# Late tiles of attention and the first Fourier products: sums, differences and splits put at other places

## The chip, the core and the metric

The kernel runs on one core of a Trainium2 chip. The metric is the device time of one execution in microseconds (us), from the first instruction of the core to the last, with what the launch adds around them. Lower is better. Five engines work side by side, each through its own queue in order: TensorE (PE; its weight loads are listed as PEld), VectorE (DVE), ScalarE (ACT), GpSimd (POOL), and SyncE (SP), which here issues the DMAs.

## What is computed

Four layers on `x` of 2048 rows and 640 columns, all in float32: attention, Fourier mixing, attention, Fourier mixing.

```python
def _A_ref(x, wqkv, wo):            # 32 heads of 20 columns
    q, k, v = split(x @ wqkv)
    scores = q @ k.T * 20 ** -0.5   # masked to 0 <= i - j < 256
    return softmax(scores) @ v @ wo
def _B_ref(x, seq_re, seq_im, hid_re, hid_im):
    a, b = x @ hid_re.T, x @ hid_im.T
    return seq_re @ a - seq_im @ b
x = x + _A_ref(_layernorm(x), wqkv, wo)
x = x + _B_ref(_layernorm(x), ...)
x = x + _A_ref(_layernorm(x), wqkv, wo)
x = x + _B_ref(_layernorm(x), ...)
```

## The kernel before

**Numbers in two parts.** A float32 operand of a matmul is split into an upper part (ACT copies it to a shorter format, L176) and a lower part (the difference, on DVE or POOL, L182; helper `split`). A product is then three matmuls: upper times upper, upper times lower, lower times upper. So every operand costs one instruction on ACT and one on DVE or POOL before PE can use it.

**The end of attention.** After the heads the output projection is finished in 16 *late tiles* of 128 rows (`late`, from L1049). For each, PE makes two halves of 320 columns in two accumulator banks; DVE adds each half to the partial result (L1096), which frees its bank, then takes mean and variance (`stats`, L234 to L238, and L1102); POOL takes the inverse root (L1107), ACT normalizes (L1060, L1057), and the row block is split for the next layer (`split_x`: upper part on ACT, lower part on POOL). POOL also makes sums of two row blocks j and j + 8 (`sum1`, L1185, and `sum3`, L1189).

**The Fourier layer** multiplies the DFT matrix of the rows with the normalized `x` (`seq`; matmuls at L1407). With the matrix and `x` each cut into two by two blocks, seven products take the place of eight, so sums and differences of blocks are operands. Each of four parts of the result (two halves of the rows, real and imaginary) takes the eight blocks j = 0 to 7 in three groups of units: "a", "b" and "g". A unit needs a *block* of the DFT matrix (1024 columns by DMA, a first part p and a second part q, raw in one of few buffers) and an *x part*:

- group a: p, and the difference t1 = q - p (L1313);
- group b: q, and q - p (L1321);
- group g, the third: q, then t1 = p - t1 (L1325 or L1337), then t1 - q (L1329 or L1338); three operands, all to be split. For j below 2 in the first part both differences are on DVE; otherwise the first is on POOL (L1337).

`cut_to(n)` makes and splits the block of all units up to n, `x_to(n)` the x parts, `load_to(n)` starts the loads. `seq(n)` calls them for n + 1 first, issues the matmuls of unit n, and then calls `cut_to(n + 2)`.

In the **first part** (sb = part = 0) the units begin while late tiles are still coming: group a is taken apart into "a1" (eight units with p, 9 matmuls each) and "a2" (eight with t1, 9 each). They alternate with late tiles: 12 matmuls of 320 columns for a tile, then 9 of 512 columns for a unit. Group b there has two units "b7" of 9 matmuls, two "b5" of 6, and six "b" of 15. Group g has eight of 21. The x part of a b unit needs the sums of `sum4_to` (two instructions on DVE, L1197 and L1198, for each j), made when `x_to` comes to it.

**What sets the order.** The program is written out in one pass. `post(d, f)` holds f back until the d-th tick after, and ticks come with the matmuls issued (`spend`). So the place of an instruction in its engine's queue is fixed at build; at run time an engine waits at its head. The last heads run under `poll_late(n)`, with n = 15 at their last step.

The ring of eight places for split blocks begins with four slices of `qp[1]`, which holds queries of the last heads until then.

Of the kernel before, what the change touches and what calls it, by code (L numbers as in the profile page):

```python
# [7 lines left out]
F32 = mybir.dt.float32  # L8
# [3 lines left out]
AF = mybir.ActivationFunctionType  # L12
OP = mybir.AluOpType
# [12 lines left out]
NB = S // P  # L26
# [31 lines left out]
def cuts(ap, n):  # L58

    return [ap[:, i:i + n] for i in range(0, ap.shape[1] - n + 1, n)]  # L60
# [6 lines left out]
class Net:  # L67
# [956 lines left out]
    def poll_late(self, n):  # L1024

        if n == 1:
            self.late_w = pairs(cuts(self.qp[0][:, :4 * D], D))
            self.late_c = self.take_cc()
            spare = [t[:, :D] for t in self.late_c[:2]]
            self.late_raw = spare  # L1030
            for k in range(EARLY, KC):
                self.nc.sync.dma_start(spare[k - EARLY], self.a["wo"][:, k, :])
        if 3 <= n < 7:
            (hi, lo), r = self.late_w[(n - 3) // 2], self.late_raw[(n - 3) // 2]
            cs = slice(n % 2 * 320, n % 2 * 320 + 320)
            self.split(hi[:, cs], lo[:, cs], r[:, cs])
        if n == 4:
            self.take_fourier()
            self.load_to(1)
        if n == 15:  # L1040
            self.cut_to(0)
        sb = len(self.late_o)
        if (n > 6 and sb < NSB and (NQ - 1, sb) in self.stored and (self.after or sb < 3)
                and (sb < 3 or self.late_t >= 3) and not (0 < sb < 3 and self.late_o[-1].get("scaled", 0) < KC - EARLY)):
            self.late_load()
# [5 lines left out]
    def late(self, xsrc, xdst, hook):  # L1051
        nc = self.nc
# [28 lines left out]
        for t in range(NB):  # L1081
            sb, i = t // 4, t % 4
            y = self.y_part(t)
# [7 lines left out]
            else:  # L1091
                for hf, cs in enumerate(both):
                    p = self.bank("o", 320)
# [26 lines left out]
            if t == NB - 2:  # L1120
                u = self.last_a2 - 1
                self.post(3, lambda u=u: self.staged(u, 0, nc.vector))
                self.post(6, lambda u=u: self.staged(u, 1))
                self.post(9, lambda u=u: self.staged(u, 2))
            hook(t)
            self.late_t = t + 1
            yield 0
# [86 lines left out]
    def take_fourier(self):  # L1214
        def halves(t):
            return t.rearrange("p (l c) -> p l c", l=2)
# [13 lines left out]
                      for ph, j in (first if sb + part == 0 else  # L1230
                                    [(ph, j) for ph in ("a", "b", "g") for j in range(half)])]
        self.kept = {}
        self.raw_of, self.cut_of, self.x_of = {}, {}, {}
        self.n_raw, self.n_load, self.n_cut, self.n_x = 0, 0, 0, 0
        self.ring = deque((t[:, 0], t[:, 1]) for t in [halves(t) for t in cuts(self.qp[1], 1024)])
        self.free = deque([0, 1, 2, 3, 4, 7])
        self.un, self.normed, self.n_sum = 0, 0, 0
        self.acc = {}
# [48 lines left out]
    def cut_to(self, n):  # L1287
        nc = self.nc
        while self.n_cut <= min(n, len(self.order) - 1):
# [17 lines left out]
            def cut(x, out=out):  # L1307
                c = self.ring.popleft()
                self.ring.append(c)
                self.split(c[0], c[1], x)  # L1310
                out.append(c)
            if ph in ("a", "a1"):
                (nc.vector if first else nc.gpsimd).tensor_tensor(out=t1, in0=q, in1=p, op=OP.subtract)  # L1313
                src = [p] + ([t1] if ph == "a" else [])
            elif ph == "a2":
                src = [t1]
            elif ph == "b5":
                self.cut_of[u] = [self.kept.pop(j)]
                continue
            elif ph == "b":  # L1320
                nc.vector.tensor_tensor(out=p, in0=q, in1=p, op=OP.subtract)  # L1321
                src = [q, p]
            elif first and j < 2:
                cut(q)
                nc.vector.tensor_tensor(out=t1, in0=p, in1=t1, op=OP.subtract)  # L1325
                cut(t1)

                def rest(p=p, q=q, t1=t1, cut=cut):
                    nc.vector.tensor_tensor(out=p, in0=t1, in1=q, op=OP.subtract)  # L1329
                    cut(p)  # L1330
                if j == 0:
                    self.rest_g = rest
                else:
                    rest()
                src = []
            else:
                nc.gpsimd.tensor_tensor(out=t1, in0=p, in1=t1, op=OP.subtract)  # L1337
                nc.vector.tensor_tensor(out=p, in0=t1, in1=q, op=OP.subtract)  # L1338
                src = [q, t1, p]
# [4 lines left out]
    def x_to(self, n):  # L1344
        nc = self.nc
        while self.n_x <= min(n, len(self.order) - 1):
# [23 lines left out]
            if ph == "g":  # L1370
                if first and j == 0:
                    self.xring = [self.work.tile([P, 2, D], F32R, name="xc", tag="wc") for _ in range(2)]
                x = [self.xring[j % 2], self.vq[j % 2].rearrange("p (l c) -> p l c", l=2)]
                self.parts(x[0], b, 0)
                self.parts(x[1], a[:, :256], 0)
            self.x_of[u] = x

    def seq(self, n):
# [46 lines left out]
            mul("m4", x[0], 384, 256, c[2])  # L1425
        soon = last and ph == "b" and not sb + part
        if soon:
            self.gather(sb, part, ph)
            self.rest_g()
            self.x_to(n + 2)  # L1430
        self.cut_to(n + 2)
        if last and not soon:
# [435 lines left out]
```

## Time and profile before

| what | value |
|---|---|
| median of 3 runs | 2134.83 us (2133.2 to 2140.98) |
| the profiled execution | 2135.22 us |
| its span, first to last instruction | 2133.2 us |
| granted clock of PE | 0.999 |
| busy: DVE | 1592.4 us, 75% |
| busy: ACT | 1149.4 us, 54% |
| busy: POOL | 854.3 us, 40% |

So 2.0 us of the profiled execution lie outside its span. In the timeline a row gives start, duration, engine, line, operation, output and inputs, shapes, and the count of merged instructions; in brackets stands how long the engine had been idle before it and what ended that. In the chain a row gives start, duration, engine, tile and line. Starts are what to count with: a new matmul starts before the one ahead of it has left the array, so the distance of two starts is the rate, and the duration is longer.

The code in question runs twice: once in the second layer (about 500 to 650 us) and once in the fourth (about 1560 to 1710 us).

### The profile page before, as it was taken

The page shows a single profiled execution, that of the slowest core. Times are in us where ns is not written, and L with a number is a line of the kernel's source. Part 1 is how long each engine was busy: PE and PEld are TensorE (multiplying, and loading weights), DVE is VectorE, ACT ScalarE, POOL GpSimd, SP SyncE. Part 2 cuts the span into 40 slices and gives each one's busy share as a digit, 9 for nine tenths or more (in the row PEclk, how much of TensorE's full clock was granted, in tenths as well). Part 3 has the DMA queues.
Part 4 walks back from the last instruction along what each step waited for, and adds up shares of the span by engine and source line. Part 5 has one row for each costly group of instructions (what it writes and reads, how often), then busy time and mean ns, then how long its engine had stood idle before and what let it go on. Part 6 is the DMA issues. An engine that isn't in the chain of part 4 may idle for free.

```text
span 2133.2 us, 45011 instructions
## 1 busy us (share of the span) xinstructions
PE 2089.0 (98%) x16405; PEld 1737.8 (81%) x16405; DVE 1592.4 (75%) x3936; ACT 1149.4 (54%) x2511; POOL 854.3 (40%) x975
## 2 busy tenths in 40 slices
PE   8999999999999999999999999999999999999999
PEld 7987776677778888889999877776777788888899
DVE  7448788777887968777751588887788868788787
ACT  3228877766554545543431288787755545445432
POOL 2036666864432324130230466668633334241300
PEclk9999999999999999999999999999999999999999
DMA  6556667876346454667645566778753364556653
GB/s 211 169 150 208 203 202 214 237 234 194 129 123 192 139 168 136 226 202 248 216 142 186 148 201 210 207 221 247 226 189 126 120 194 123 183 161 201 231 173 121
DMA packets 220061, 395.12 MB, mean 185 GB/s; under 512 B 37824, under 2 KB 84416, under 8 KB 219840
## 3 DMA queue, kind: packets, MB, share of 16 engines
q1 hardware_dynamic: 219840, 392.25, 59.3%
q8 instruction: 129, 2.11, 0.4%
q14 instruction: 92, 0.75, 0.1%
HBM read 273.94 MB, written 117.05 MB: 183 GB/s over the span
## 4 chain that ended last, share of the span: by engine, by line
PE 81%; DVE 6%; POOL 4%; DMA 4%; ACT 3%; issue 1%; SPq 0%; ACTq 0%; POOLq 0%; DVEq 0%
PE banks L1407 29%; PE banks L189 15%; PE banks L207 13%; PE banks L703 7%; PE banks L1662 7%; PE banks L661 5%; PE banks L629 5%; DMA rr<-r_d 1%; POOL big L182 1%; POOL ou L1337 1%; DVE banks L634 1%; DVE qp L182 1%; PE banks L289 1%; ACT big L1057 1%; DMA pt<-c 1%
## 5 line engine op out<-in xcount | busy, mean ns | idle before, releaser
L634 DVE CUSTOM_DVE_ANT_0 banks<-banks,mask 128x384 f32<-128x384 f32 (+2 forms) x1024 | 513.8, 565 | 147.7 <-PE banks L629 119.0
L672 ACT ACTIVATE pt<-banks 128x384 f32<-128x384 f32 (+2 forms) x864 | 359.7, 472 | 74.1 <-PE banks L629 32.7
L629 PE MATMUL banks<-kp,qp 60*128 60x384 f32 (+2 forms) x1024 | 336.7, 368 | 4.7 <-DVE mc L634 2.9
L207 PE MATMUL banks<-big,wc 64*128 64x512 f32 x1920 | 337.0, 396 | 0.4 <-DVE pt L422 0.4
L661 PE MATMUL banks<-qp,kp 61*128 61x384 f32 (+2 forms) x1024 | 334.4, 362 | 2.7 <-DMA qp<-mt 1.1
L629 PEld LDWEIGHTS banks<-kp,qp 60*128 60x128 f32 x1024 | 172.0, 184 | 59.6 <-DVE mc L634 44.0
L661 PEld LDWEIGHTS banks<-qp,kp 61*128 61x128 f32 x1024 | 176.6, 185 | 41.7 <-ACT pt L672 16.0
L686 POOL TENSOR_SCALAR_AFFINE_SELECT pt<-pt 128x512 f32<-128x512 f32 x216 | 138.3, 640 | 172.4 <-ACT pt L672 142.4
L207 PEld LDWEIGHTS banks<-big,wc 64*128 64x128 f32 x1920 | 196.5, 187 | 12.2 <-DVE pt L422 0.5
L1337 POOL TENSOR_TENSOR pt<-pt,pt 128x512 f32<-128x512 f32 x36 | 62.0, 1721 | 288.7 <-DMA pt<-c 148.9
L176 ACT ACTIVATE cc<-pt 128x512 fp32r<-128x512 f32 x150 | 93.9, 626 | 153.9 <-POOL pt L1313 52.5
L703 PE MATMUL banks<-pt,vq 128*32 128x128 f32 (+1 forms) x3664 | 172.0, 311 | 3.7 <-POOL pt L686 3.7
L176 ACT ACTIVATE qp<-pt 128x512 fp32r<-128x512 f32 (+1 forms) x195 | 119.8, 624 | 93.4 <-DVE pt L1338 45.6
L182 DVE TENSOR_TENSOR cc<-pt,cc 128x512 fp32r<-128x512 f32 x150 | 121.4, 820 | 52.0 <-ACT cc L176 49.7
L182 DVE TENSOR_TENSOR qp<-pt,qp 128x512 fp32r<-128x512 f32 (+1 forms) x195 | 151.7, 791 | 10.5 <-ACT qp L176 7.9
L1407 PE MATMUL banks<-qp,big 128*128 128x512 f32 x630 | 151.1, 391 | 5.0 <-DVE qp L182 4.0
L703 PEld LDWEIGHTS banks<-pt,vq 128*32 128x32 f32 x3664 | 97.6, 109 | 60.4 <-issue 16.9
L634 DVE DVE_READ_ACCUMULATOR2_ANT mc<- 128x1 f32 x1024 | 144.6, 141 | 0.0
L1407 PEld LDWEIGHTS banks<-qp,big 128*128 128x128 f32 x630 | 117.0, 188 | 31.1 <-DVE qp L182 5.7
L690 POOL TENSOR_SCALAR_AFFINE_SELECT pt<-pt 128x512 f32<-128x512 f32 x190 | 123.0, 648 | 0.0
L1407 PE MATMUL banks<-qp,xc 128*128 128x512 f32 x480 | 117.9, 390 | 1.8 <-DVE xc L182 1.5
L1407 PEld LDWEIGHTS banks<-qp,xc 128*128 128x128 f32 x480 | 89.8, 188 | 22.2 <-DVE xc L182 2.3
(240 smaller groups left out, 4529.1 us busy)
## 6 DMA issues: line engine op xcount, KB each, us to landing
pt<-c SPq DMA_DIRECT2D x188, 512.0 KB
kp<-qk_d SPq DMA_DIRECT2D x128, 160.0 KB
qp<-qk_d SPq DMA_DIRECT2D x128, 160.0 KB
kp<-u_d SPq DMA_DIRECT2D x32, 640.0 KB
o_d<-ou SPq DMA_DIRECT2D x64, 256.0 KB
x_d<-x SPq DMA_DIRECT2D x48, 320.0 KB
v_d<-pt SPq DMA_DIRECT2D x16, 768.0 KB
qk_d<-cc SPq DMA_DIRECT2D x24, 512.0 KB
```

What stands on the lines that cost most here:

```text
L176: nc.scalar.activation(hi, src, AF.Copy, scale=-1.0 if neg else 1.0)
L182: (eng or nc.vector).tensor_tensor(out=lo, in0=src, in1=hi.bitcast(F32), op=OP.subtract)
L189: self.nc.tensor.matmul(p, x, y, start=n == 0, stop=n == last)
L207: self.nc.tensor.matmul(ps[a], x[r], y[r], start=half + i == 0, stop=half == 1 and i == n - 1, skip_group_check=True)
L629: nc.tensor.matmul(p, qp[quad % 2][b:b + 60, z, qb * P:(qb + 1) * P], kp[quad % 2][b:b + 60, z, k0 * P:(qb + 1) * P], start=True, stop=True)
L634: nc.vector.tensor_tensor_reduce(out=p, in0=p, in1=self.mask[:, 384 - n * P:], scale=1.0, scalar=NEG, op0=OP.add, op1=OP.max, accum_out=mc ...
L661: nc.tensor.matmul(self.banks[:, tb[e], :n * P], kp[quad % 2][b:b + 61, z, kb * P:(kb + 1) * P], qp[quad % 2][b:b + 61, z, kb * P:(kb + n) ...
L672: nc.scalar.activation(pt[quad, kb][:, 2 * z + e, :n * P], self.banks[:, tb[e], :n * P], AF.Exp, scale=SCALE)
L686: nc.gpsimd.affine_select(out=t[:, :, 0:P], in_=t[:, :, 0:P], pattern=[[0, h], [1, P]], compare_op=OP.is_ge, fill=0.0, base=0, channel_mul ...
L703: nc.tensor.matmul(p[32 * h:32 * h + 32, (c0 - qa) * P:(c1 - qa) * P], vq[:, 96 * (kb % 4) + 21 * h:96 * (kb % 4) + 21 * h + 32], t[:, h, ...
L1407: nc.tensor.matmul(self.banks[:, bk, :], p, b[q], start=start and m == 0, stop=stop and last and m == 2, skip_group_check=True)
L1662: nc.tensor.matmul(bank[to], a, b, start=start and n == 0, stop=stop and n == last, skip_group_check=True)
```

## The change

It touches only the late tiles and the first part of each Fourier layer.

1. At the last step of the heads `cut_to(1)` takes the place of `cut_to(0)`, so the blocks of the first two a1 units are split there. The ring takes the slices of `qp[1]` in the order 0, 2, 1, 3.
2. The first two differences t1 (j = 0 and 1) are not made there: they are kept in `put_off` and posted with late tiles 7 and 8.
3. The sums of `sum4_to` for j = 0 to 4 are posted with late tiles 8 to 12; for j = 5 to 7 they stay in `x_to`.
4. In group g of the first part all differences are on DVE, for every j (before, POOL made the first one from j = 2 on). The upper parts are issued with new helpers `upper` (ACT) and `lower` (DVE), and in another order: both differences are queued before the second lower part.
5. In group g the x part of unit n + 2 is issued ahead of the block of unit n + 2, at the end of `seq(n)`. At the end of group b, the x part of the second g unit has its upper parts issued ahead of the sums that gather group b, and its lower parts (`rest_x`) behind the rest of the first g block.

```diff
         if n == 15:
-            self.cut_to(0)
+            self.cut_to(1)
...
                 self.post(9, lambda u=u: self.staged(u, 2))
+            if 0 <= t - NB // 2 < 5:
+                self.post(9, lambda j=t - NB // 2: self.sum4_to(j + 1))
+            if t in (7, 8,):
+                self.post(9, self.put_off.pop(0))
             hook(t)
...
-        self.ring = deque((t[:, 0], t[:, 1]) for t in [halves(t) for t in cuts(self.qp[1], 1024)])
+        self.ring = deque((t[:, 0], t[:, 1]) for t in [halves(cuts(self.qp[1], 1024)[i]) for i in (0, 2, 1, 3)])
...
+            def upper(x, out=out):
+                c = self.ring.popleft()
+                self.ring.append(c)
+                nc.scalar.activation(c[0], x, AF.Copy)
+                out.append(c)
+
+            def lower(i, x, out=out):
+                nc.vector.tensor_tensor(out=out[i][1], in0=x, in1=out[i][0].bitcast(F32), op=OP.subtract)
             if ph in ("a", "a1"):
-                (nc.vector if first else nc.gpsimd).tensor_tensor(out=t1, in0=q, in1=p, op=OP.subtract)
+                def less(j=j, t1=t1, p=p, q=q, first=first):
+                    (nc.vector if first else nc.gpsimd).tensor_tensor(out=t1, in0=q, in1=p, op=OP.subtract)
+                    if first:
+                        self.lessened.add(j)
+
+                if first and j < 2:
+                    self.put_off.append(less)
+                else:
+                    less()
...
-            elif first and j < 2:
-                cut(q)
+            elif first:
+                upper(q)
+                lower(0, q)
                 nc.vector.tensor_tensor(out=t1, in0=p, in1=t1, op=OP.subtract)
-                cut(t1)
-
-                def rest(p=p, q=q, t1=t1, cut=cut):
-                    nc.vector.tensor_tensor(out=p, in0=t1, in1=q, op=OP.subtract)
-                    cut(p)
+                upper(t1)
+                nc.vector.tensor_tensor(out=p, in0=t1, in1=q, op=OP.subtract)
+                lower(1, t1)
+                upper(p)
                 if j == 0:
-                    self.rest_g = rest
+                    self.rest_g = lambda p=p, lower=lower: lower(2, p)
                 else:
-                    rest()
+                    lower(2, p)
                 src = []
...
-                self.parts(x[0], b, 0)
-                self.parts(x[1], a[:, :256], 0)
+                for d, y in zip(x, (b, a[:, :256])):
+                    if not (first and j == 1):
+                        self.parts(d, y, 0)
+                    else:
+                        nc.scalar.activation(d[:, 0], y, AF.Copy)
+                        self.rest_x.append(lambda d=d, y=y: nc.vector.tensor_tensor(
+                            out=d[:, 1], in0=y, in1=d[:, 0].bitcast(F32), op=OP.subtract))
...
         if soon:
+            self.rest_x = []
+            self.x_to(n + 2)
             self.gather(sb, part, ph)
             self.rest_g()
+            for f in self.rest_x:
+                f()
+        if ph == "g" and not sb + part and j in (0,1,2,3,4,5,):
             self.x_to(n + 2)
         self.cut_to(n + 2)
```

In the changed kernel the lines move: L1313 becomes L1328, L1197 and L1198 become L1201 and L1202, L1321 becomes L1344, L1337 becomes L1360, L1407 becomes L1435, L1456 becomes L1489; the lower parts of group g stand at L1325, and its two differences at L1349 and L1351.

In the listings of the order below, a row is one instruction in an engine's queue (line, operation, output and inputs, shape of the output, and a count where equal ones follow); minus is before only, plus is changed only. `pt_96` and `vq_92` are places of t1, `s_6559` and `s_6560` raw blocks (later sums), `cc`, `rr` and `qp_102` places of split blocks, `xc` and `vq` of x parts.

## The prediction on record

> **What bounds the kernel now.** I read the page first: span, busy shares and chain.
>
> ```profile
> span 2133.2 us, 45011 instructions
> PE 2089.0 (98%) x16405; PEld 1737.8 (81%) x16405; DVE 1592.4 (75%) x3936; ACT 1149.4 (54%) x2511; POOL 854.3 (40%) x975
> PE 81%; DVE 6%; POOL 4%; DMA 4%; ACT 3%; issue 1%; SPq 0%; ACTq 0%; POOLq 0%; DVEq 0%
> ```
>
> TensorE is the bound, so only its stalls can be won: 2133.2 - 2089.0 = 44 us, and a few tenths after each restart that count as busy. The edits lie where the chain leaves PE. So next came PE's timeline over the first Fourier part in the second layer, with only the rows that matter kept:
>
> ```profile
> 517.23 2.45 PE L1407 MATMUL banks<-qp,big 128*128 128x512 f32 x10
> 520.99 2.11 PE L1407 MATMUL banks<-qp,big 128*128 128x512 f32 x8 [1.31 <-DVE qp L182]
> ...
> 535.35 2.03 PE L189 MATMUL banks<-qp,kp 128*128 128x320 f32 x12 [0.78 <-DVE x L1096]
> ...
> 569.17 0.73 PE L1407 MATMUL banks<-qp,big 128*128 128x512 f32 x2 [0.72 <-DVE qp L182]
> ...
> 575.27 2.21 PE L1407 MATMUL banks<-qp,big 128*128 128x512 f32 x9
> ...
> 603.88 2.20 PE L1407 MATMUL banks<-qp,xc 128*128 128x512 f32 x9
> ...
> 646.43 3.79 PE L1407 MATMUL banks<-qp,big 128*128 128x512 f32 x16
> ```
>
> and the same places in the fourth layer:
>
> ```profile
> 1634.84 2.20 PE L1407 MATMUL banks<-qp,big 128*128 128x512 f32 x9
> ...
> 1663.45 2.20 PE L1407 MATMUL banks<-qp,xc 128*128 128x512 f32 x9
> ...
> 1706.65 1.52 PE L1407 MATMUL banks<-qp,big 128*128 128x512 f32 x6
> ```
>
> Last, the chain in order of time, for the rate when nothing waits and for what stands behind the worst stall of the third group:
>
> ```profile
> 614.10 4.33 DMA pt<-c
> 618.56 3.63 POOL ou L1337
> 622.21 1.77 DVE pt L1338
> 627.67 264.87 PE banks L1407 x1167
> ```
>
> An unhindered 512-column matmul takes 264.87 / 1167 = 0.227 us. From 575.27 to 603.88 PE issues 9 + 9 + 2 x 6 + 6 x 15 = 120 matmuls: 27.24 us of work in 28.61, so **1.37 us lost in group b**; the fourth layer (1634.84 to 1663.45) loses the same. Group g has 8 x 21 = 168: 38.14 us in 42.55 (603.88 to 646.43), so **4.41 lost in group g**, and 43.20 - 38.14 = 5.06 in the fourth layer. The second unit should have started at 517.23 + 10 x 0.227 = 519.50 and came at 520.99: 1.49 lost.
>
> **Part 1: the second unit's block, split within the heads.** DVE's queue behind the late tiles, at the start of the second unit:
>
> ```order
>  L1102 TENSOR_SCALAR nb<-mv 128x1
> -L1313 TENSOR_TENSOR pt_96<-s_6560 128x512
> -L182 TENSOR_TENSOR qp_102<-s_6560,qp_102 128x512
> -L1313 TENSOR_TENSOR pt_96<-pt_95 128x512
> +L1328 TENSOR_TENSOR pt_96<-pt_95 128x512
>  L182 TENSOR_TENSOR qp_102<-pt_95,qp_102 128x512
> ```
>
> Two instructions are gone from here; inside the heads one L182 takes the place of one L1313. Their price, and what a late tile costs DVE:
>
> ```profile
> 519.12 1.21 DVE L1313 TENSOR_TENSOR pt<-s 128x512 f32<-128x512 f32 x1
> 520.25 0.68 DVE L182 TENSOR_TENSOR qp<-s,qp 128x512 fp32r<-128x512 f32 x1
> 520.86 0.68 DVE L1313 TENSOR_TENSOR pt<-pt 128x512 f32<-128x512 f32 x1
> ...
> 534.82 0.88 DVE L1096 TENSOR_TENSOR x<-banks,big 128x320 f32<-128x320 f32 x2
> ...
> 536.97 0.68 DVE L1313 TENSOR_TENSOR pt<-pt 128x512 f32<-128x512 f32 x1
> 537.57 0.68 DVE L182 TENSOR_TENSOR cc<-pt,cc 128x512 fp32r<-128x512 f32 x1
> ...
> 540.92 1.51 DVE L182 TENSOR_TENSOR cc<-pt,cc 128x512 fp32r<-128x512 f32 x1
> 542.36 0.88 DVE L1096 TENSOR_TENSOR x<-banks,big 128x320 f32<-128x320 f32 x2
> ...
> 548.61 0.81 DVE L182 TENSOR_TENSOR qp<-pt,qp 128x512 fp32r<-128x512 f32 x1 [0.90 <-ACT qp L176]
> 549.34 0.88 DVE L1096 TENSOR_TENSOR x<-banks,big 128x320 f32<-128x320 f32 x2
> ...
> 561.04 0.88 DVE L1096 TENSOR_TENSOR x<-banks,big 128x320 f32<-128x320 f32 x2
> ```
>
> From 519.12 to 520.86 the two take 1.74 us; with the collision that a later L1313 avoids I take 2.0 (1.7 to 2.1). The rows up to 542.36 bear no bracket, that is, no idle time ahead of them, so all of DVE's work there comes 2.0 earlier. PE's stall at 520.99 goes (1.49), and of the one at 535.35, which waits for DVE's L1096, what makes 2.0 together. The upper part that moves into the heads is one more ACT instruction in their last step; ACT is busy 54% of the span, and I cost it at nothing. Uncovered, it would be of the size of DVE's 0.68 for as many columns.
>
> **Part 2: differences and sums behind late tiles.** DVE's queue at tiles 8 to 10:
>
> ```order
>  L182 TENSOR_TENSOR cc<-pt_95,cc 128x512
> +L1328 TENSOR_TENSOR pt_96<-s_6559 128x512
> +L1096 TENSOR_TENSOR x<-banks,big_5491 128x320 x2
> +L234 BN_STATS st<-x 128x6 x2
> +L236 BN_AGGR mv<-st 128x2
> +L238 TENSOR_SCALAR rs<-mv 128x1
> +L1102 TENSOR_SCALAR nb<-mv 128x1
> +L182 TENSOR_TENSOR cc<-pt_96,cc 128x512
> +L1201 TENSOR_TENSOR big_5460<-big_5460 128x256
> +L1202 TENSOR_TENSOR kp_7441<-big_5491,big_5460 128x256
> +L1328 TENSOR_TENSOR pt_96<-s_6560 128x512
>  L1096 TENSOR_TENSOR x<-banks,big_5491 128x320 x2
> ```
>
> Each of five tiles gets a pair of sums, two of them a difference as well, all ahead of the next L1096, which frees the bank that the next late tile's matmuls need. A difference is 0.60 (536.97 to 537.57). The pair, from group b's rows:
>
> ```profile
> 577.09 0.42 DVE L1197 TENSOR_TENSOR big<-big 128x256 f32<-128x256 f32 x1
> 577.54 0.43 DVE L1198 TENSOR_TENSOR kp<-big,big 128x256 f32<-128x256 f32 x1
> 577.88 0.42 DVE L1197 TENSOR_TENSOR big<-big 128x256 f32<-128x256 f32 x1
> ```
>
> is 0.79. DVE waits 0.90 per tile for ACT here (548.61), so alone the pair would fit. But POOL is busy at the same time:
>
> ```profile
> 540.35 1.53 POOL L182 TENSOR_TENSOR big<-big,big 128x384 fp32r<-128x384 f32 x1 [1.51 <-ACT big L176]
> ...
> 548.13 0.74 POOL L1185 TENSOR_TENSOR big<-big,big 128x256 f32<-128x256 f32 x1 [0.65 <-ACT big L1057]
> 549.44 0.74 POOL L182 TENSOR_TENSOR big<-big,big 128x256 fp32r<-128x256 f32 x1 [0.57 <-ACT big L176]
> ```
>
> At 540.92 DVE's L182 took 1.51 instead of 0.68 while POOL's L182 ran, until 541.88: it waited for POOL's whole instruction. At 548.61 it took 0.81, for the 0.13 that L1185 (until 548.87) still had. By the Trainium skill, page "SBUF — State Buffer", section "Who interferes with whom", a DVE instruction with two SBUF inputs contends with a GpSimd one that reads SBUF, and the lock is held for the whole instruction; the 1.51 agrees. By that rule a late tile pays up to 0.74 for each meeting; by the 0.13 alone the sum would be that of the first rival.
>
> POOL's L182 (549.44) is ready just as DVE's L182 ends, where the sums now stand. So I count one POOL instruction waited out per tile: 2.15 for L1096 and statistics (534.82 to 536.97), 0.60, 0.79 and 0.74 make 4.28, against (561.04 - 549.34) / 3 = 3.90 now. Five tiles: 5 x 0.38 = 1.9. Late tiles in sum: -2.0 + 2 x 0.60 + 1.9 = **+1.1 per layer, +2.2 in all**. PE follows, since the stall at 569.17 waits for DVE behind the last tile and moves with it. Ends: -1.8 per layer, if the pairs stay in the 0.90 and the differences in what is left of it (0.11 a tile, all 0.90 in tiles without a pair), and +9.9, if each of DVE's three (0.60, 0.79 in two) waits out 0.74 (5.76 a tile, 9.3 over five) and each difference too (1.3 each), less 2.0. I take one wait: the rows fix the time of that meeting, and of no other.
>
> **Part 3: group b without five of eight sums.** DVE loses 3 x 0.79 = 2.4 us ahead of the b5 units and one pair in each of the next two b units, whose matmuls take 15 x 0.227 = 3.41. Now a b unit costs DVE 3.59:
>
> ```profile
> 586.86 0.42 DVE L1197 TENSOR_TENSOR big<-big 128x256 f32<-128x256 f32 x1
> ...
> 590.45 0.42 DVE L1197 TENSOR_TENSOR big<-big 128x256 f32<-128x256 f32 x1
> ```
>
> Without a pair it is 2.80; the three units that keep one cost 0.18 too much each, less than the lead won. So of the 1.37 I take 1.25: **-2.5 in both layers** (ends 0 and -2.7).
>
> **Part 4: group g.** DVE's queue before, for the unit j = 4:
>
> ```order
> L182 TENSOR_TENSOR xc<-big_5491,xc 128x640
> L182 TENSOR_TENSOR vq_7796<-big_5460,vq_7796 128x256
> L1338 TENSOR_TENSOR pt_93<-ou_97,pt_93 128x512
> L182 TENSOR_TENSOR cc<-pt_93,cc 128x512
> L182 TENSOR_TENSOR cc<-ou_97,cc 128x512
> L182 TENSOR_TENSOR rr<-pt_93,rr 128x512
> ```
>
> and in the changed kernel, for the same unit:
>
> ```order
> L182 TENSOR_TENSOR xc<-big_5491,xc 128x640
> L182 TENSOR_TENSOR vq_7806<-big_5460,vq_7806 128x256
> L1325 TENSOR_TENSOR cc<-pt_93,cc 128x512
> L1349 TENSOR_TENSOR ou_97<-pt_93,ou_97 128x512
> L1351 TENSOR_TENSOR pt_93<-ou_97,pt_93 128x512
> L1325 TENSOR_TENSOR cc<-ou_97,cc 128x512
> L1325 TENSOR_TENSOR rr<-pt_93,rr 128x512
> ```
>
> POOL's difference, for which DVE's waited (618.56 and 622.21 in the chain), is gone; the first lower part needs only the load. DVE does one more:
>
> ```profile
> 601.23 0.82 DVE L182 TENSOR_TENSOR xc<-big,xc 128x640 fp32r<-128x640 f32 x1
> 601.96 0.42 DVE L182 TENSOR_TENSOR vq<-big,vq 128x256 fp32r<-128x256 f32 x1
> 602.30 0.68 DVE L182 TENSOR_TENSOR qp<-pt,qp 128x512 fp32r<-128x512 f32 x1
> ...
> 604.29 0.69 DVE L182 TENSOR_TENSOR qp<-pt,qp 128x512 fp32r<-128x512 f32 x1 [0.70 <-ACT qp L176]
> ```
>
> By the starts 0.73 + 0.34 + 5 x 0.60 = 4.07 us a unit against 21 x 0.227 = 4.77 on PE. The wait of 0.70 for ACT's upper part goes, since the second difference is queued into it. The x part now stands ahead on ACT and waits until PE has left the unit two back, with the block behind it: all must be done in one unit's 4.77. With 0.70 for ACT's start, the first lower part is there after 0.70 + 1.07 + 0.60 = 2.37; the third, needed only 15 matmuls (3.41) into the unit, after 0.70 + 4.07 = 4.77: it holds. The load at 614.10 began when the last lower part of an older unit had freed its buffer; that part now comes earlier, and 4.33 fits into one unit. I leave 0.25 per layer for what is late next: -4.15 and -4.8, **-9.0** (ends +1.7, the second rival, and -9.5).
>
> **Sum.** +2.2 - 2.5 - 9.0 = -9.3. From the profiled execution's 2135.2 (span 2133.2 and 2.0 around it) that is 2125.9; from the median, 0.4 lower, 2125.5, which I predict. A measurement of this kernel tells about 0.5% (10.7 us) from no change, so the forecast itself, -6 to -11.6, is mostly "the same": 0.45.
>
> **Rivals.**
> - *The sums fit into DVE's wait.* For it: the L182 at 548.61 ran beside POOL and took 0.81 only, and 0.79 is less than 0.90. Against: the 1.51. Late tiles -1.8 per layer: -3.6 - 2.5 - 9.0 = -15.1, 2119.7. Chance 0.23.
> - *DVE becomes the bound of group g.* If both hand-overs to ACT stay, 4.07 + 1.40 = 5.47 per unit, 0.70 over PE's 4.77; over eight units 5.6, in place of 4.41 and 5.06: +1.7 instead of -9.0. It decides once the waits pass 0.70 a unit. Against: the order now puts the second difference into the wait. +1.4, 2136.2. Chance 0.09.
> - *Half of the stalls of b and g come back behind another wait* (a load, or DVE's start into group g). For: DMA, POOL and DVE follow one another in the chain there, so one gone may uncover the next. -5.7 + 2.2 = -3.5, 2131.3. Chance 0.17.
> - *Slower: VectorE and GpSimd alternate at every instruction in tiles 8 to 12.* Place and price as the upper end of part 2, 9.9 per layer: +19.8 - 11.5 = +8.3, 2143.1. It passes the gain (5.75 a layer) once a late tile takes over 5.2 us, (5.75 + 0.8) / 5 = 1.3 more than now. For: 1.51, and POOL's 1.53 at 540.35. Against: the 0.81 at 548.61. Beside it stands the Trainium skill's rule of part 2 ("SBUF — State Buffer", "Who interferes with whom"), if the lock goes to the other engine after each instruction; no run shown here has that. Chance 0.06.
>
> Faster by over 0.5%: most of the first rival (0.21) and the third of the forecast beyond -10.7 (0.15), 0.36. Slower by over 0.5%: half of the last, 0.03. Same: the rest, 0.61. The range 2118.5 to 2134.0 reaches over the first and third rivals; above it lie the last (0.06) and most of the second (0.07), below it some 0.06.
>
> **What would show it.** Right: no PE stall at the second unit; L1096 about 4.3 us apart in tiles 9 to 13, DVE's new sums at 1.1 and more beside POOL's; b units 3.41 apart; no stall over 0.3 in group g, 168 matmuls in about 38.4; L1360 absent from the first part. Wrong: tiles still 3.9 apart (first rival); g units 5 us and more apart (second); a PE wait for DMA or DVE at the start of group g (third); tiles over 5.2 us apart (last).

## The result and the profile after

| | before | changed |
|---|---|---|
| median of 6 runs each | 2135.91 us (2133.2 to 2140.98) | 2124.97 us (2122.72 to 2126.36) |
| ratio, with its 95% interval | | 0.9947 (0.9936 to 0.9959) |
| profiled execution, span | 2133.2 us | 2123.0 us |

The changed kernel is 10.9 us faster, 0.53%. The interval, 0.41 to 0.64%, lies across the bound of 0.5%, so the runs don't decide between "faster" and "the same" in the prediction's sense; the time itself came 0.5 us beside the 2125.5 forecast. That it came so near is in part luck: with three more runs the median of the kernel before rose from 2134.83 to 2135.91, so the gain is 1.6 more than the 9.3 forecast.

The head of the page shows TensorE as busy as before, in a span 10.2 shorter:

```profile
span 2123.0 us, 44985 instructions
PE 2086.9 (98%) x16405; PEld 1740.9 (82%) x16405; DVE 1596.6 (75%) x3948; ACT 1149.6 (54%) x2511; POOL 832.7 (39%) x963
```

PE's timeline in the second layer, at the places that the prediction showed of before (first unit, a late tile that waits for DVE, the stall behind the last tile, last a2 unit, group b, start and end of group g):

```profile
514.75 4.27 PE L1435 MATMUL banks<-qp,big 128*128 128x512 f32 x18
...
530.85 2.02 PE L189 MATMUL banks<-qp,kp 128*128 128x320 f32 x12 [0.37 <-DVE x L1096]
...
566.85 0.73 PE L1435 MATMUL banks<-cc,big 128*128 128x512 f32 x2 [0.35 <-DVE cc L182]
...
572.95 2.21 PE L1435 MATMUL banks<-qp,big 128*128 128x512 f32 x9
...
583.29 0.84 PE L1435 MATMUL banks<-rr 128*128 128x512 f32 x3
...
586.69 0.84 PE L1435 MATMUL banks<-qp,rr 128*128 128x512 f32 x3
...
600.29 2.20 PE L1435 MATMUL banks<-qp,xc 128*128 128x512 f32 x9
...
638.59 8.32 PE L1435 MATMUL banks<-qp,big 128*128 128x512 f32 x36
```

and in the fourth layer:

```profile
1572.48 4.27 PE L1435 MATMUL banks<-qp,big 128*128 128x512 f32 x18
...
1630.68 2.21 PE L1435 MATMUL banks<-qp,big 128*128 128x512 f32 x9
...
1658.02 2.20 PE L1435 MATMUL banks<-qp,xc 128*128 128x512 f32 x9
...
1696.10 4.24 PE L1435 MATMUL banks<-qp,big 128*128 128x512 f32 x18
```

The eighteen matmuls at 514.75 are the first two units in one row: the stall at the second unit (1.31) is gone. Units of group b start 3.40 apart (583.29, 586.69). Distances of these starts give the three stages. "Late" runs from the first unit to the last a2 unit, "b" from there to the first matmul of group g, "g" from there to the next part:

| us, second / fourth layer | late | b | g |
|---|---|---|---|
| before | 58.05 / 58.01 | 28.61 / 28.61 | 42.55 / 43.20 |
| changed | 58.20 / 58.20 | 27.34 / 27.34 | 38.30 / 38.08 |
| difference | +0.15 / +0.19 | -1.27 / -1.27 | -4.25 / -5.12 |
| forecast | +1.1 / +1.1 | -1.25 / -1.25 | -4.15 / -4.8 |

Together -11.6. The rest of each Fourier layer, behind group g, is 0.4 longer (in the second layer 0.28 of it are two matmuls at 649.2 and 649.5 that start late, which none does in the kernel before), so from its first to its last matmul a Fourier layer is 4.95 and 5.82 shorter: 10.8 in all, near the 10.9 between the medians. Outside, only the last step of the heads differs (part 1). From the start of PE's last row of L703, a matmul of the heads, to the first unit it took 14.52 and 14.53 before and takes 14.55 in both layers now, so the block that is split there, costed at nothing, did cost next to nothing. All the rest has the same instructions in both kernels and scatters by itself: over all profiled executions of this study PE's first unit began at 513.4 to 517.4 (before: 517.23, changed: 514.75), and from the end of group g to the first unit of the fourth layer it took 930.4 to 938.8 (before: 930.4, changed: 933.9). So small effects are read from the stages below, which repeat within 0.1 (g within 0.3), and the whole times are only asked to agree.

### The profile page after: what moved, and what is told of

The parts are those of the page before. It is cut to its first block, busy times and chain, and to the rows that moved or that the text cites. A ratio compares the mean times of both kernels' runs of the same rounds, so it can differ in the third digit from the quotient of the medians.

```text
span 2123.0 us, 44985 instructions
## 1 busy us (share of the span) xinstructions
PE 2086.9 (98%) x16405; PEld 1740.9 (82%) x16405; DVE 1596.6 (75%) x3948; ACT 1149.6 (54%) x2511; POOL 832.7 (39%) x963
## 5 line engine op out<-in xcount | busy, mean ns | idle before, releaser
L672 ACT ACTIVATE pt<-banks 128x384 f32<-128x384 f32 (+2 forms) x864 | 359.8, 472 | 74.2 <-PE banks L629 38.1
L703 PE MATMUL banks<-pt,vq 128*32 128x128 f32 (+1 forms) x3664 | 171.5, 311 | 4.4 <-POOL pt L686 4.3
L176 ACT ACTIVATE cc<-pt 128x512 fp32r<-128x512 f32 x136 | 84.9, 627 | 142.6 <-POOL pt L1328 53.5
L182 DVE TENSOR_TENSOR cc<-pt,cc 128x512 fp32r<-128x512 f32 x136 | 114.5, 845 | 49.4 <-ACT cc L176 46.9
L1435 PE MATMUL banks<-qp,big 128*128 128x512 f32 x630 | 148.5, 390 | 0.0
L176 ACT ACTIVATE qp<-pt 128x512 fp32r<-128x512 f32 (+1 forms) x173 | 105.4, 624 | 78.8 <-DVE pt L1361 41.4
L703 PEld LDWEIGHTS banks<-pt,vq 128*32 128x32 f32 x3664 | 97.8, 109 | 60.5 <-issue 17.5
L1435 PEld LDWEIGHTS banks<-qp,big 128*128 128x128 f32 x630 | 117.5, 188 | 23.6
L182 DVE TENSOR_TENSOR qp<-pt,qp 128x512 fp32r<-128x512 f32 (+1 forms) x173 | 128.0, 757 | 5.1 <-ACT qp L176 3.3
L1360 POOL TENSOR_TENSOR pt<-pt,pt 128x512 f32<-128x512 f32 x30 | 45.3, 1510 | 203.7 <-DMA pt<-c 95.4
L1328 POOL TENSOR_TENSOR pt<-pt 128x512 f32<-128x512 f32 x30 | 46.3, 1547 | 186.6 <-ACT cc L1321 124.6
L1435 PE MATMUL banks<-qp,xc 128*128 128x512 f32 x480 | 115.3, 389 | 0.0
```

The source lines that it names most:

```text
L176: nc.scalar.activation(hi, src, AF.Copy, scale=-1.0 if neg else 1.0)
L182: (eng or nc.vector).tensor_tensor(out=lo, in0=src, in1=hi.bitcast(F32), op=OP.subtract)
L672: nc.scalar.activation(pt[quad, kb][:, 2 * z + e, :n * P], self.banks[:, tb[e], :n * P], AF.Exp, scale=SCALE)
L703: nc.tensor.matmul(p[32 * h:32 * h + 32, (c0 - qa) * P:(c1 - qa) * P], vq[:, 96 * (kb % 4) + 21 * h:96 * (kb % 4) + 21 * h + 32], t[:, h, ...
L1435: nc.tensor.matmul(self.banks[:, bk, :], p, b[q], start=start and m == 0, stop=stop and last and m == 2, skip_group_check=True)
```

## The experiments

Each was run beside the kernel before, on the same chip. All results stand in one table, "sum" being the three stages of both layers less those of the changed kernel (247.5). It doesn't hold what happens ahead of the first unit: there two kernels differ from the others, as told with "differences early".

| kernel | late | b | g | sum | ratio to before |
|---|---|---|---|---|---|
| changed, again | 58.20 / 58.18 | 27.34 / 27.35 | 38.29 / 38.38 | +0.3 | 0.9951 (0.9938 to 0.9963) |
| no sums late | 56.58 / 56.58 | 28.56 / 28.57 | 38.92 / 38.89 | +0.6 | 0.9952 (0.9940 to 0.9965) |
| three pairs late | 57.45 / 57.44 | 28.32 / 28.31 | 38.95 / 38.95 | +2.0 | 0.9954 (0.9941 to 0.9968) |
| second block late | 59.59 / 59.56 | 27.38 / 27.34 | 38.31 / 38.29 | +3.0 | 0.9960 (0.9948 to 0.9972) |
| differences early | 57.90 / 57.88 | 27.33 / 27.33 | 38.33 / 38.38 | -0.3 | 0.9952 (0.9939 to 0.9965) |
| old group g | 58.18 / 58.21 | 27.39 / 27.35 | 42.45 / 41.91 | +8.0 | 0.9977 (0.9967 to 0.9986) |
| no x part ahead | 58.18 / 58.20 | 27.39 / 27.35 | 40.67 / 40.42 | +4.7 | 0.9964 (0.9952 to 0.9976) |
| POOL's difference | 58.21 / 58.22 | 27.35 / 27.33 | 38.75 / 38.76 | +1.2 | 0.9959 (0.9947 to 0.9971) |
| new order alone | 58.19 / 58.22 | 27.37 / 27.34 | 40.92 / 40.96 | +5.5 | 0.9979 (0.9969 to 0.9988) |
| x part ahead alone | 58.22 / 58.22 | 27.34 / 27.34 | 41.00 / 40.57 | +5.2 | 0.9961 (0.9949 to 0.9974) |
| three pairs, early norm | 56.99 / 56.97 | 28.31 / 28.32 | 38.91 / 38.91 | +1.0 | 0.9956 (0.9943 to 0.9968) |
| five pairs, both edits | 57.40 / 57.40 | 27.34 / 27.35 | 38.08 / 38.33 | -1.6 | 0.9948 (0.9936 to 0.9961) |

### What the sums behind late tiles cost and bring

**No sums late.** The five pairs go back into group b:

```diff
-            if 0 <= t - NB // 2 < 5:
-                self.post(9, lambda j=t - NB // 2: self.sum4_to(j + 1))
```

> The changed kernel without part 2's sums: all eight pairs of sums are made in the b units again; all else as changed. Stretches by PE's starts in the second layer, changed kernel: late 58.20 us (first a1 unit to last a2 unit), b 27.34, g 38.30. Theory W (the sums cost the chain POOL, ACT, POOL of each tile, which they hold up at the lock, about 0.4 us for each of five tiles; DVE's own time lies in its wait for ACT): late falls to 56.2, b goes back to 28.6, g stays; together -0.7 per layer, 2123.5 us. Theory N (the sums cost nothing there, and part 1's 2.0 us were lost to the two differences): late stays at 58.0 or more, b 28.6: +1.2 per layer, 2127.5 us.

Late tiles came down by 1.62 a layer, 0.32 for a pair on average and nearly as far as theory W had it. But b rose by 1.22, and g, which W left where it was, by 0.6 and 0.8: the late place is 0.3 per layer better on balance. So the pairs do cost a third of a microsecond each beside POOL, and their place as a whole is worth almost nothing. DVE's rows in the changed kernel, from the late tile behind which PE first waits to the one behind the last pair:

```profile
530.31 0.88 DVE L1096 TENSOR_TENSOR x<-banks,big 128x320 f32<-128x320 f32 x2
...
538.45 0.88 DVE L1096 TENSOR_TENSOR x<-banks,big 128x320 f32<-128x320 f32 x2
...
543.14 0.89 DVE L1096 TENSOR_TENSOR x<-banks,big 128x320 f32<-128x320 f32 x2
...
547.17 0.88 DVE L1096 TENSOR_TENSOR x<-banks,big 128x320 f32<-128x320 f32 x2
...
551.07 0.88 DVE L1096 TENSOR_TENSOR x<-banks,big 128x320 f32<-128x320 f32 x2
...
553.39 0.81 DVE L182 TENSOR_TENSOR qp<-vq,qp 128x512 fp32r<-128x512 f32 x1 [0.16 <-ACT qp L176]
554.13 0.41 DVE L1201 TENSOR_TENSOR big<-big 128x256 f32<-128x256 f32 x1
554.58 0.84 DVE L1202 TENSOR_TENSOR kp<-big,big 128x256 f32<-128x256 f32 x1
555.34 0.88 DVE L1096 TENSOR_TENSOR x<-banks,big 128x320 f32<-128x320 f32 x2
...
559.62 0.88 DVE L1096 TENSOR_TENSOR x<-banks,big 128x320 f32<-128x320 f32 x2
...
561.94 0.81 DVE L182 TENSOR_TENSOR cc<-ou,cc 128x512 fp32r<-128x512 f32 x1 [0.17 <-ACT cc L176]
...
563.28 0.48 DVE L1096 TENSOR_TENSOR x<-banks,big 128x320 f32<-128x320 f32 x1
```

and POOL's split beside them:

```profile
554.19 0.95 POOL L182 TENSOR_TENSOR big<-big,big 128x256 fp32r<-128x256 f32 x1 [0.53 <-ACT big L176]
```

Between 538.45 and 559.62 a pair stands ahead of each L1096. The tile with the first pair, and a difference, takes 4.69, the next two 4.03 and 3.90, and the last two 4.27 and 4.28 (551.07, 555.34, 559.62). In these last two L1202 takes 0.84 where it takes 0.43 alone, and POOL's L182 0.95 in place of 0.74: each waited for the other once. By the Trainium skill, page "SBUF — State Buffer", section "Who interferes with whom", the two share a port pair under an exclusive lock, held for the instruction; the rows agree, with one change of hands per tile (L1201, POOL's L182, L1202). DVE's wait for ACT, 0.90 before, is down to 0.16.

**Three pairs late.** Only j = 0 to 2 stay behind tiles (`< 3` in place of `< 5`).

> The pairs of sums for j = 3 and 4 go back into group b; those for j = 0 to 2 stay behind late tiles. Taking all five back shortened the late tiles by 1.6 us per layer (58.2 to 56.6) and cost 1.2 in group b and 0.7 in group g. Theory (a pair costs about 0.3 where it stands behind a late tile, and group b needs DVE's lead only for its first units): late tiles about 57.5, group b 27.3 to 27.6, group g 38.1 to 38.6; 0.3 to 0.6 less per layer than the changed kernel, so about 1 us faster than it. Rival (every pair's place in group b costs what it saves in the late tiles, and group g starts with a smaller lead): late tiles 57.5, group b 27.9, group g 38.7, no gain or up to 0.6 per layer slower.

The rival held, and the result is worse than it: late 0.75 less, but b at 28.32 and g at 38.95. Two pairs in group b cost 0.98; the three others had cost next to nothing there (28.56 with none late, 28.32 with three). Why, DVE's rows ahead of the b5 blocks show, here with three pairs late:

```profile
577.58 0.76 DVE L182 TENSOR_TENSOR qp<-kp,qp 128x256 fp32r<-128x256 f32 x2 [1.28 <-ACT qp L176]
...
580.71 0.69 DVE L182 TENSOR_TENSOR cc<-pt,cc 128x512 fp32r<-128x512 f32 x1 [1.16 <-ACT cc L176]
...
585.71 0.42 DVE L1201 TENSOR_TENSOR big<-big 128x256 f32<-128x256 f32 x1
...
589.31 0.42 DVE L1201 TENSOR_TENSOR big<-big 128x256 f32<-128x256 f32 x1
```

The same place in the kernel before, where the three pairs (577.09 to 579.48) stand:

```profile
579.48 0.75 DVE L182 TENSOR_TENSOR qp<-kp,qp 128x256 fp32r<-128x256 f32 x2
...
581.85 0.69 DVE L182 TENSOR_TENSOR cc<-pt,cc 128x512 fp32r<-128x512 f32 x1 [0.42 <-ACT cc L176]
```

With the pairs gone DVE waits there for ACT, 1.28 + 1.16 in place of 0.42; most of the 2.4 us of sums (3 x 0.79) were covered by that. From then on, with a pair in each unit, DVE needs 3.60 a unit (585.71 to 589.31) and PE follows at that rate. The pairs j = 3 and 4 are those that pay: without them the first two long units need only 2.80 of DVE (3.60 less a pair's 0.79), and its lead lasts to group g. A kernel with j = 0 to 2 in group b and only j = 3 and 4 behind late tiles follows from this; it wasn't run.

### The second block and the put-off differences

**Second block late.** The first part of the change undone, the differences still put off:

```diff
-            self.cut_to(1)
+            self.cut_to(0)
...
-        self.ring = deque((t[:, 0], t[:, 1]) for t in [halves(cuts(self.qp[1], 1024)[i]) for i in (0, 2, 1, 3)])
+        self.ring = deque((t[:, 0], t[:, 1]) for t in [halves(t) for t in cuts(self.qp[1], 1024)])
```

> The changed kernel without part 1: only the first unit's block is split in the heads, the ring in its old order. Theory of the prediction: the stall before the second unit is back (1.5 us), DVE's queue is 2.0 us longer up to tile 9 and all behind it moves: late 60.2, b and g unchanged, +4 us in all, 2129 us. Rival (the late stretch ends on ACT and POOL anyway, with slack in it): the stall comes back but late grows by 0.5 at most, 2126 us.

Late 59.6, 1.4 more: between the two. PE's stall comes back at half its size, since the block's difference, put off, no longer stands ahead of it:

```profile
516.78 2.46 PE L1435 MATMUL banks<-qp,big 128*128 128x512 f32 x10
519.93 2.11 PE L1435 MATMUL banks<-qp,big 128*128 128x512 f32 x8 [0.69 <-DVE qp L182]
```

The L1096 that DVE began 17.59 after the first unit before, and 15.56 after it in the changed kernel, comes 16.96 after it here. So of the 2.0 in DVE's queue the block's lower part is 1.4, and the other 0.6 is its difference, which went away from there.

**Differences early.** They are made at the heads again:

```diff
-            if t in (7, 8,):
-                self.post(9, self.put_off.pop(0))
...
-                if first and j < 2:
-                    self.put_off.append(less)
-                else:
-                    less()
+                less()
```

> The first two differences of group a are not put off to late tiles 7 and 8 but made where the block is split, at the last step of the heads and before the first late tiles. Theory: two DVE instructions of 0.60 leave tiles 7 and 8, which wait for DVE, and stand ahead of the first tiles, which wait for PE; the late tiles, from the first unit's start, take 57.6 to 57.9 in place of 58.2. Rival 1 (they only change places, since the tiles behind wait for DVE's queue as a whole): late tiles 58.2, within 0.1. Rival 2 (the place at the heads costs PE a stall at the second unit): a stall of 0.5 or more there, late tiles 58.5 and over.

Late 57.90, as the theory had it, and no stall at the second unit. But this stage begins with the first unit, and what the edit moved lies ahead of it. There PE now waits for one L1096 more, behind the two differences:

```profile
502.41 0.86 PE L703 MATMUL banks<-pt,vq 128*32 128x128 f32 x24
...
506.81 1.14 PE L189 MATMUL banks<-qp,kp 128*128 128x320 f32 x6 [0.27 <-DVE x L1096]
...
517.43 4.27 PE L1430 MATMUL banks<-qp,big 128*128 128x512 f32 x18
```

The row of L703 in the changed kernel, whose first unit starts at 514.75:

```profile
500.20 0.86 PE L703 MATMUL banks<-pt,vq 128*32 128x128 f32 x24
```

From that row to the first unit it is 15.02 here, and 15.03 in the fourth layer, for 14.55 in both layers of the changed kernel. The early differences take 0.31 off the stage and put 0.47 on ahead of it: with the block split inside the heads, putting them off saves some 0.15 a layer.

### What makes group g faster

**Old group g.** Parts 1 to 3 of the change stay, parts 4 and 5 go:

```diff
-            elif first:
-                upper(q)
-                lower(0, q)
...
+            elif first and j < 2:
+                cut(q)
...
-        if ph == "g" and not sb + part and j in (0,1,2,3,4,5,):
-            self.x_to(n + 2)
```

> Parts 1 to 3 alone: group g, its x parts and the gathering before it in the old order, POOL making the first difference from j = 2 on. Theory of the prediction (group g's gain is the new order's): g back near 42.5 us in the second layer and 43.2 in the fourth, late 58.2, b 27.3: +9 us over the changed kernel, 2134 us. Rival (the gain in g comes from the lead that DVE wins in group b): g at most 39.5, 2127.5 us or less.

g is back at 42.45 and 41.91. The edits inside it bring 4.15 and 3.8; the 0.1 and 1.3 that remain came with parts 1 to 3.

**No x part ahead.** The new order stays, the last two lines of the diff above go.

> The changed kernel without the call that makes the x part of unit n + 2 ahead of its block in group g (j = 0 to 5). Theory O (the place of the differences does the work; the x part keeps its distance to PE either way, since it waits for the unit two back): g 38.3 to 38.6, 2125 us. Theory X (the x part behind the block is what made PE wait for xc): two to four stalls of 0.6 us per layer come back, g 40 to 41, 2129 us.

g 40.67 and 40.42: the x part's place is worth 2.35 of some 4. PE's longest wait of that stage, and, one fence further, ACT's queue behind it:

```profile
612.25 2.76 PE L1435 MATMUL banks<-rr,xc 128*128 128x512 f32 x9 [1.02 <-ACT xc L176]
```

```profile
610.13 0.63 ACT L1321 ACTIVATE cc<-pt 128x512 fp32r<-128x512 f32 x1 [1.44 <-DVE pt L1349]
610.94 0.63 ACT L1321 ACTIVATE qp<-pt 128x512 fp32r<-128x512 f32 x1 [0.17 <-DVE pt L1351]
611.48 0.72 ACT L176 ACTIVATE xc<-big 128x640 fp32r<-128x640 f32 x1
```

In the changed kernel ACT has it here, ahead of the block that waits for DVE's differences:

```profile
606.88 0.72 ACT L176 ACTIVATE xc<-big 128x640 fp32r<-128x640 f32 x1
...
610.04 0.63 ACT L1321 ACTIVATE cc<-pt 128x512 fp32r<-128x512 f32 x1 [1.60 <-DVE pt L1349]
```

The x part needs nothing of DVE; behind the block it waited out the block's 1.44 and 0.17 on ACT first.

**POOL's difference.** All as changed, but `(nc.vector if j < 2 else nc.gpsimd)` makes L1349.

> All as changed, but in group g of the first part the first difference (t1 = p - t1) is on POOL again for j from 2 on; the new order and the x part ahead stay. Theory A (the move of the difference from POOL to DVE is what removed the stalls): group g goes back to 41 to 42.5 us from 38.2. Theory B (the order is what removed them; POOL's 3.6 us fit, since it may begin as soon as the block has landed): group g at 38.2 to 39.5, DVE with 0.6 less per unit, the whole within 2 us of the changed kernel. With the x part behind the block, the run without x ahead, group g was 40.5.

g 38.75, theory B: 0.5 and 0.7 more. POOL's difference now takes 1.3 to 1.8 us and the 3.63 of before doesn't recur. DVE, with 0.72 less to do in a unit, loses that again where the two meet; a row of POOL's, and DVE's L1325 that ran into it:

```profile
613.05 1.51 POOL L1349 TENSOR_TENSOR ou<-pt,ou 128x512 f32<-128x512 f32 x1 [5.02 <-DMA pt<-c]
```

```profile
613.33 1.78 DVE L1325 TENSOR_TENSOR qp<-pt,qp 128x512 fp32r<-128x512 f32 x1
```

**New order alone** (this and the edit before together) and **x part ahead alone** (old group g, with the two lines of `x_to(n + 2)` put back):

> Group g with the new order, but with the first difference on POOL (from j = 2 on) and without the x part ahead. So far group g took 42.2 us with all as before, 40.5 without the x part ahead, 38.75 with POOL's difference, 38.2 as changed. Theory (the parts work one by one): 40.5 + 0.55 = 41.0 to 41.3, and the new order by itself is worth 1 us. Rival (POOL's 1.3 to 1.8 us are hidden only while the x part is ahead): 42 or more, the new order by itself is worth nothing.

> Group g with the old order and POOL's first difference, and only the x part issued ahead of the block. Theory 1 (the x part's place is the main part by itself, since PE waited for an x part in the run without it): group g 39.5 to 40.5. Theory 2 (it needs the new order too: the x part ahead holds up DVE and ACT, which wait for PE to leave the unit two back, and the old order then has its differences behind that): 41.5 to 44.

The order alone, with POOL's difference: 40.9, a little under the theory's 41.0 to 41.3. The x part alone: 41.00 and 40.57, between the two theories. So the order takes 1.5 and 0.95 off by itself, the x part 1.45 and 1.34, and both with POOL's difference 3.7 and 3.15, more than the sum. (The order of the x part at the end of group b is counted with the new order; it wasn't tried by itself.) With the x part alone the old order's waits are what is left:

```profile
611.89 1.45 PE L1418 MATMUL banks<-cc,xc 128*128 128x512 f32 x5 [0.54 <-DVE cc L182]
...
614.17 2.12 PE L1418 MATMUL banks<-rr,xc 128*128 128x512 f32 x8 [0.60 <-DVE rr L182]
```

```profile
608.84 0.69 DVE L182 TENSOR_TENSOR cc<-pt,cc 128x512 fp32r<-128x512 f32 x1 [0.70 <-ACT cc L176]
...
610.83 1.01 DVE L182 TENSOR_TENSOR cc<-pt,cc 128x512 fp32r<-128x512 f32 x1 [0.70 <-ACT cc L176]
```

In the first two units, where both differences are on DVE, it waits 0.70 twice a unit for ACT's copy of a difference that it has just made. PE's stalls come from this lateness, and none is left behind 614.17; the new order puts the second difference into the wait.

### A version with two edits more

**Three pairs, early norm.** As with three pairs late, and the norm of the last but one late tile two ticks earlier (`d = 1 if t == NB - 2 else 0` in place of `d = 3`).

> The kernel with three pairs of sums behind late tiles, and besides the norm of the last but one late tile issued two ticks earlier, ahead of the last tile's statistics. In the changed kernel ACT and POOL have three waits at the end of the late tiles (0.35, 0.50 and 1.01 us on PE). Theory: the split of the last but one tile is ready earlier and one of these waits (0.5) goes; late tiles about 57.0, 0.3 to 0.5 less per layer than with three sums alone. Rival (the last unit waits for the last tile, which comes no earlier): late tiles the same as with three sums alone, within 0.1, or up to 0.3 longer, since the last statistics stand behind.

Late 56.99, 0.46 less, as the theory had it. PE's three waits at the end (0.48, 0.50 and 1.02 with three pairs) have become one:

```profile
566.15 2.10 PE L1435 MATMUL banks<-cc,big 128*128 128x512 f32 x8 [1.75 <-DVE cc L182]
```

**Five pairs, both edits.** The changed kernel with that and the differences early; and **the changed kernel again** beside it:

> The changed kernel with the two edits that shortened the late tiles elsewhere: the norm of the last but one late tile two ticks earlier (it took 0.46 us off per layer) and the first two differences made at the heads (0.31 off). Theory (they add up, as they sit at other places): late tiles 57.4, group b 27.35, group g 38.3: 1.6 us less than the changed kernel over both layers. Rival (with five sums the last tiles are late by DVE, and the norm's early place gains nothing): late tiles 57.9, 0.6 us less over both layers.

> The changed kernel once more, unaltered, to stand beside the others on one chip. If the stages repeat: late tiles 58.2, group b 27.35, group g 38.1 to 38.3 in both layers, and a ratio to the kernel before within 0.994 to 0.996.

Late 57.40: in this stage the two add up, 0.8 per layer, and the stages are 1.6 us shorter than the changed kernel's in total. But ahead of the first unit the early differences cost their 0.47 here too (15.02 in both layers), so 0.6 of the 1.6 is left, and that gain is the norm's. The whole times don't tell the two apart (medians 2126.53 and 2126.47, ratios 0.9948 and 0.9951), as they can't at this size.

## Why the prediction was right, and where it was not

**Late tiles: +1.1 per layer forecast, +0.15 and +0.19 measured; the one term that was mis-sized.** Its own steps held, in sum, until the last. From each kernel's first unit, L1096 came at 17.59 before (534.82 - 517.23) and 15.56 in the changed kernel: -2.03 for the forecast -2.0. The row of tile 14 stands at 561.04 - 517.23 = 43.81 before and 559.62 - 514.75 = 44.87 now: +1.06. So the differences and pairs cost DVE the 3.1 forecast. The pairs didn't cost it evenly, though: by the distances of L1096 in both kernels the first cost 0.98, the others 0.16, -0.02, 0.36 and 0.41, and that these add up to the 1.9 of five times 0.38 is luck. The step that failed is "PE follows, since the stall at 569.17 waits for DVE behind the last tile and moves with it". Between tile 14's L1096 and the last tile's lay one more wait for ACT, in a step that bears no pair. Before:

```profile
564.19 0.81 DVE L182 TENSOR_TENSOR cc<-ou,cc 128x512 fp32r<-128x512 f32 x1 [0.91 <-ACT cc L176]
...
565.53 0.47 DVE L1096 TENSOR_TENSOR x<-banks,big 128x320 f32<-128x320 f32 x1
```

Now it is 0.17 (561.94), and the step takes 3.66 in place of 4.49. ACT hadn't moved with DVE (its copy for this step began 46.31 after the first unit before and 46.54 now), so the lost time was given back there. The prediction named such waits only in its lower bound and its first rival.

The 4.28 of a tile with a pair was met by the last two of the five, but with other parts. One POOL instruction waited out at 0.74 was forecast; measured were 0.43 of waiting in the sums, 0.14 left in L182 (0.74 to the next start in place of 0.60) and 0.17 of the wait for ACT. These come to the same 0.74 by accident. "About 4.3 apart in tiles 9 to 13" was thus a sign that only some tiles showed.

**Group b: -1.25 forecast, -1.27 measured, for one of its two reasons.** The pairs taken out of the two long units pay, as reckoned at 2.80 against 3.41 a unit. The 2.4 us ahead of the b5 units, counted as DVE's loss, had for the most part stood inside a wait for ACT.

**Group g: -4.15 and -4.8 forecast, -4.25 and -5.12 measured.** 168 matmuls take 38.1 to 38.3, and L1360 is absent from the first part. The weights of the reasons were wrong. POOL's difference, named first as the stall that goes, is 0.5 to 0.7; the x part's place, named only as a risk, is the largest single part (2.35 taken away by itself). The order, named for the 0.70, comes next: 2.25 and 1.81, from "x part ahead alone" to "POOL's difference". A unit on DVE is not 4.07 but 4.48, since three of its steps use a result just made, or ACT's copy of one, and start later for it:

```profile
613.20 0.69 DVE L1325 TENSOR_TENSOR qp<-pt,qp 128x512 fp32r<-128x512 f32 x1
613.80 0.69 DVE L1349 TENSOR_TENSOR vq<-pt,vq 128x512 f32<-128x512 f32 x1
614.52 0.69 DVE L1351 TENSOR_TENSOR pt<-vq,pt 128x512 f32<-128x512 f32 x1
615.18 0.69 DVE L1325 TENSOR_TENSOR qp<-vq,qp 128x512 fp32r<-128x512 f32 x1
615.97 0.69 DVE L1325 TENSOR_TENSOR qp<-pt,qp 128x512 fp32r<-128x512 f32 x1
...
617.68 0.69 DVE L1325 TENSOR_TENSOR cc<-pt,cc 128x512 fp32r<-128x512 f32 x1
```

That is from 613.20 to 617.68; the three starts behind the first difference lie 0.72, 0.66 and 0.79 apart, not 0.60. It stays under PE's 4.77, so it cost nothing.

**The rivals.** Sums that fit into DVE's wait: not for most: one pair in five fitted in (3.90), and the late tiles as a whole came out between (+0.15, for the forecast's +1.1 and this rival's -1.8). DVE as the bound of g: no, 4.48. Half the stalls back: no; 0.4 per layer came back in the next part. DVE and POOL alternating at every instruction: they do change hands, once a tile, at 0.4 to 0.5 for DVE, far below the 1.3 a tile from which it decides.

**The sum.** -9.3 forecast, -10.8 over the Fourier layers: the late tiles' 1.9 less than feared and g's 0.4 more, less 0.8 given back in the next part. Taken apart by the runs, of the -11.6 in the stages group g is 8.0, the second block 3.0 and the sums 0.6. The put-off differences cost 0.6 in the late tiles of both layers and save 0.9 ahead of them. Each part was taken away by itself, so they don't have to add up.

## What to carry to other kernels

Follow a delay on one engine to the last wait ahead of the bound: if that wait is for an engine that the change doesn't move, it gives the delay back. Work on an engine that waits a moment later for another is free where it stands, so before moving it away, look at whether that wait simply grows by as much. Queue an operand that depends on nothing ahead of a chain that passes between two engines, and fill the hand-over of that chain with the next independent step; the two together brought more than the sum of each by itself. And begin the stage that you measure ahead of everything that an edit moves: the early differences looked like a gain only in a stage that began behind them.

## What the runs showed of the hardware

- A meeting of VectorE and GpSimd costs both a part: the 128x256 sum 0.84 to 0.97 for 0.43, GpSimd's 128x256 split 0.95 to 1.27 for 0.74.
- Here a 128x512 VectorE operation takes 0.69 either way, but the next start lies 0.60 behind it when it is independent and 0.66 to 0.79 when it uses the result or waits for ScalarE's copy of it.
- TensorE's three waits of 0.48, 0.50 and 1.02 in a row came to more than the one of 1.75 that took their place: the stage was 0.46 shorter, 0.25 of it idle time. Where the other 0.21 lies the rows don't show.
